# Expert 0's first row numbers from one-hot matmuls, and the later lists read behind the gathers, in a fused attention and mixture-of-experts kernel

## The chip, the cores and the metric

The kernel runs on one core of one Trainium2 chip. The metric is the device time of one execution in microseconds; a program is judged by the median of its runs. TensorE (PE) multiplies matrices, with its weight load written PEld; VectorE is DVE, ScalarE is ACT, GpSimd is POOL, and SyncE (SP) issues the plain DMAs. Each engine works through its own instructions strictly in order, so an instruction that waits holds up everything behind it on that engine.

## The reference, cut to what matters

```python
x = attention(q, k, v)                      # 2304 tokens of 512
x = relu(x @ w_in) ** 2 @ w_out             # dense layer, 512 -> 2048 -> 512
logits = x @ w_gate                         # 8 experts
e_idx = argmax(logits, axis=1)              # one expert for each token
gate_w = softmax(logits)[e_idx]
eom = 1 / (1 + exp(-(x @ w_output_gate)))
for e in range(8):
    mask = e_idx == e
    h = relu(x[mask] @ w1[e])               # 512 -> 1024
    out[mask] = gate_w[mask] * eom[mask, e] * (h @ w2[e])
```

With the inputs used here the experts 0 to 7 get 87, 361, 162, 89, 231, 520, 500 and 354 tokens.

## The kernel before, in words

Attention comes first, then the dense layer in nine chunks of 256 tokens, and behind each chunk its routing (`routing(c)`): the chosen expert, the token's rank in that expert and the gate value. Every token's result row of 520 numbers, gate included, is written to a table in DRAM (`ytab`, line 607). Its row number (`row`, 1 to 2304) is scattered to a place in DRAM lists (`orders`, line 601, two lists, one for the even and one for the odd 128 tokens of a chunk; both start as zeros, so their sum is the list). Expert e's list begins at place 2304e; `sc[:, 5, :]` holds each token's place as a float.

The expert stage needs the rows of one expert gathered in tiles of 128. One expert is chosen early as the lead (`star`, the fullest one after seven chunks; here expert 5). Its first FT = 2 tiles are gathered with the lists as they stand before the last chunk (`lead_rows`, called at step f = 6 of the last chunk) and are worked on as `fill` work (`lead_1` is layer 1, `lead_2` turns the hidden values and runs layer 2) while the last chunk's routing runs. `fill` is driven in steps of one matmul.

After the last routing, lines 958 to 973 read expert 0's list back from DRAM (`c4`), add the two lists (`cf`), step over the lead's two tiles if expert 0 should be the lead (`cd`, `star`), make integers (`ci`), and gather expert 0's first two tiles (`xg01`). Lines 979 to 983 and 999 to 1021 read all lists (`og`), turn them on TensorE (`po`) and make the integer places of all further tiles (`gi`). Line 996 holds the first three weight loads of expert 1 on SP behind the `c4` DMAs. `ph1.close()` gives up the buffers of the first phase, and the tiles of pool `mp2`, weight stages 3 to 7 among them, lie in that memory.

Then the loop over experts (line 1108): layer 1 of the tile in `xs0`, the weights of the next expert converted to two parts and loaded, rows of the next tiles gathered (`gather`, line 1041), turned and split (`split_rows`), the hidden values turned (`hand_over`), and at the end `tc.If(nt[e] > 1)` (line 1155). Where an expert has one tile, as expert 0 has, the other branch is taken. The first tile of the next expert (`xgs[0]`) is gathered by line 1097 before the loop. Layer 2 of a tile runs behind layer 1 of the next.

The instruction order on each engine is set ahead of time by a scheduler that simulates the program; `tc.high_priority()` moves work forward in it, and `tc.issue_after(x)` keeps instructions behind x on x's engine.

Of the kernel before, what the change touches and what calls it, by code (L numbers as in the profile page):

```python
# [10 lines left out]
F32 = mybir.dt.float32  # L11
F32R = mybir.dt.float32r
BF16 = mybir.dt.bfloat16
I32 = mybir.dt.int32
# [11 lines left out]
def attn_moe_kernel(  # L26
# [13 lines left out]
    nc = tc.nc  # L40
# [489 lines left out]
    def routing(c):  # L530
# [171 lines left out]
    def lead_rows():  # L702

        of = const.tile([P, 2, FT], F32, name="of")
        for i, o in enumerate(orders):
            nc.sync.dma_start(out=of[:, i, :], in_=lists(o)[bass.ds(most["e"], 1), :, 0:FT].rearrange(
                "o p t -> (o p) t"))
        oi = const.tile([P, FT], I32, name="oif")
        nc.vector.tensor_add(out=oi, in0=of[:, 0, :], in1=of[:, 1, :])
        xe = late.tile([P, FT, YW], F32, tag="xe", name="xe")  # L710
# [4 lines left out]
        most["xe"] = xe  # L715

    def lead_split():
        xs = mp.tile([P, FT, 2, DM], F32R, tag="xc", name="xsf")
# [18 lines left out]
    def lead_2(x):  # L737
# [3 lines left out]
        for h in range(2):  # L741
            t = psh.tile([P, DM], F32, tag="ph", name=f"ptf{x}_{h}")
            for c in range(4):
                f0 = 512 * h + P * c
                nc.tensor.transpose(out=t[:, P * c:P * c + P], in_=most["hr"][:, f0:f0 + P],
                                    identity=ident)
                yield
            nc.scalar.activation(out=hs[2 * h], in_=t, func=AF.Copy)
            nc.vector.tensor_sub(out=hs[2 * h + 1], in0=t, in1=hs[2 * h].bitcast(F32))
# [200 lines left out]
    for part, n in (("yt", 10), ("lg", 4), ("ps", 9)):  # L950
        route(1)
        with tc.issue_after(most[part]):
            drive(fill, n)
    route(8)


    star = most["star"]
    with tc.high_priority():
        c4 = const.tile([P, 2, 2 * FT], F32, name="c4")
        for i, o in enumerate(orders):  # L960
            got = nc.sync.dma_start(out=c4[:, i, :], in_=lists(o)[0, :, 0:2 * FT])
        cf = const.tile([P, 2 * FT], F32, name="cf")
        nc.vector.tensor_add(out=cf, in0=c4[:, 0, :], in1=c4[:, 1, :])
        cd = const.tile([P, FT], F32, name="cd")
        nc.vector.tensor_sub(out=cd, in0=cf[:, FT:], in1=cf[:, 0:FT])
        ci = const.tile([P, FT], I32, name="ci")
        nc.vector.scalar_tensor_tensor(out=ci, in0=cd, scalar=star[:, 0:1], in1=cf[:, 0:FT],
                                       op0=ALU.mult, op1=ALU.add)
        xg01 = [late.tile([P, YW], F32, tag=f"xg{i}", name=f"xg0{i}") for i in range(2)]
        for i in range(2):  # L970
            nc.gpsimd.indirect_dma_start(
                out=xg01[i][:], out_offset=None, in_=ytab[:],
                in_offset=bass.IndirectOffsetOnAxis(ap=ci[:, i:i + 1], axis=0))
# [4 lines left out]
    ogs = []  # L978
    for o in orders:
        og = cv.tile([P, DM], I32, tag="tmp", name="og", bufs=TMPB).bitcast(F32)[:E * NTL // 2, 0:2 * P]  # L980
        nc.gpsimd.dma_start(out=og.rearrange("t (h p) -> t h p", h=2),
                            in_=o.rearrange("(t h p) o -> t h (p o)", h=2, p=P))
        ogs.append(og)
    cs = counts("c")
    nti = const.tile([P, E], I32, name="nti")
    nc.vector.tensor_copy(nti, cs)
# [12 lines left out]
    po = psa.tile([P, 2, DM], F32, tag="at", name="po")  # L999
    for h in range(2):  # L1000
        for i, og in enumerate(ogs):
            with tc.issue_after(most["end"]):
                nc.tensor.matmul(po[:, 0, h * E * NTL // 2:(h + 1) * E * NTL // 2],
                                 lhsT=og[:, P * h:P * h + P],
                                 rhs=ident[:E * NTL // 2, :E * NTL // 2], start=(i == 0), stop=(i == 1))
    gi = late.tile([P, E * NTL // 2, 2], I32, tag="gi", name="gi")

    HT = NTL // 2
    pov = po[:, 0, 0:E * NTL].rearrange("p (h e j) -> p h e j", h=2, e=E)
    gih = gi.rearrange("p (e j) h -> p h e j", e=E)  # L1010
    sh = cv.tile([P, DM], F32, tag="tmp", name="sh", bufs=TMPB)[:, 0:E * (NTL - 2)].rearrange(
        "p (h e j) -> p h e j", h=2, e=E)
    nc.vector.tensor_copy(gi, po[:, 0, 0:E * NTL].rearrange("p (h t) -> p t h", h=2))
    for h in range(2):
        nc.vector.tensor_sub(out=sh[:, h], in0=pov[:, h, :, 1:HT], in1=gih[:, h, :, 0:HT - 1])
        nc.vector.tensor_tensor(out=sh[:, h], in0=sh[:, h],
                                in1=star.unsqueeze(2).to_broadcast([P, E, HT - 1]),
                                op=ALU.mult)
        nc.vector.tensor_tensor(out=gih[:, h, :, 0:HT - 1], in0=pov[:, h, :, 0:HT - 1], in1=sh[:, h],
                                op=ALU.add)  # L1020
    giv = gi.rearrange("p t h -> p (t h)")
    ph1.close()


# [9 lines left out]
    xs0 = mp2.tile([P, 2, DM], F32R, tag="xs0", name="xs0", bufs=1)  # L1034
    early[3] = mp2.tile([P, 1024], F32, tag="stg3", name="stg3", bufs=1)
    hr = most["hr"]
    g1, gn, gp = (mp2.tile([P, 2], F32, tag=f"g{i}", name=f"g{i}", bufs=1) for i in range(3))
    stages += [early[i] for i in range(3, 8)]

# [68 lines left out]
    for e in range(E):  # L1108
# [2 lines left out]
        n = f"{e}_0"  # L1111
        nt[e] = nc.values_load(nti[0:1, e:e + 1], min_val=0, max_val=NTL)
        first_mm = layer1_here(w1v, xs0, n)
        if more:
            after = experts[e + 1]
            after.place(0)
            with ExitStack() as behind:
                if e == 0:
                    for x in first_xs:
                        behind.enter_context(tc.issue_after(x))  # L1120
                for i in range(4):
                    after.split(i)
            for i in range(4, 8):
                after.load(i, stages[i])
# [99 lines left out]
```

## Time and profile before

| | us |
|---|---|
| median of 3 runs | 904.06 (900.21 to 905.27) |
| the profiled execution | 903.22 |
| its span | 901.4 |
| PE busy in the span | 821.4 (91%) |
| DVE, ACT, POOL busy | 450.6, 395.3, 341.6 |

Times in the rows are counted from the start of the span. A row of the timeline is one or more instructions of one line; the square bracket behind it is the idle time of that engine just before, and what ended it. SPq and PEq are the engines' sequencers, which run register, branch and DMA-issuing instructions; a sequencer can be ahead of its engine's array. [...]

### The profile page before, as it was taken

What the parts mean: (1) busy time and instruction counts of PE and PEld (TensorE: products, weight loads), DVE (VectorE), ACT (ScalarE), POOL (GpSimd) and SP (SyncE); (2) the same over time, 40 slices, a digit from 0 to 9 for tenths busy, and PEclk for the clock granted to TensorE, in tenths of its full rate; (3) what the DMA queues carried; (4) which work ended last, traced back from release to release, by engine and by line L of the source; (5) the groups of instructions that cost most, each with busy time, mean ns of one, the idle gap of its engine ahead of it and who ended that gap; (6) DMA issues with size and microseconds to landing.
All of it is one profiled execution on the core that took longest, in us unless ns stands there. A gap on an engine that the chain in (4) does not pass through costs nothing. (4 is left out here: it accounts for less than half of the span.)

```text
span 901.4 us, 15844 instructions
## 1 busy us (share of the span) xinstructions
PE 821.4 (91%) x5983; PEld 695.4 (77%) x5983; DVE 450.6 (50%) x961; ACT 395.3 (44%) x899; POOL 341.6 (38%) x411
## 2 busy tenths in 40 slices
PE   4598979997899989999999999997799989999996
PEld 3386869886788878888988888775587767878785
DVE  8987585777354654353222224652743656434121
ACT  3644555554434443344333324552643656444221
POOL 4556454454344445453323232413422332221111
PEclk9989989999899999999999999998899999999999
DMA  9750321454034332010000031635945594431111
GB/s 335 254 179 31 117 80 71 164 187 163 24 102 79 79 101 65 30 38 30 1 25 1 1 95 55 207 110 152 355 148 191 172 347 137 177 132 37 49 35 35
DMA packets 35519, 103.45 MB, mean 115 GB/s; under 512 B 6836, under 2 KB 6864, under 8 KB 35408
## 3 DMA queue, kind: packets, MB, share of 16 engines
q1 hardware_dynamic: 30000, 87.16, 28.9%
q0 software_dynamic: 5408, 14.88, 5.4%
q8 instruction: 61, 1.00, 0.5%
q14 instruction: 50, 0.41, 0.2%
HBM read 88.16 MB, written 14.65 MB: 114 GB/s over the span
## 5 line engine op out<-in xcount | busy, mean ns | idle before, releaser
L461 PE MATMUL ph<-xc,win 128*128 128x256 f32 x1728 | 244.6, 288 | 14.1 <-DVE g L466 11.9
L461 PEld LDWEIGHTS ph<-xc,win 128*128 128x128 f32 x1728 | 230.0, 193 | 33.4 <-DVE g L466 14.8
L484 PE MATMUL y<-wout,gs 128*128 128x512 f32 x864 | 233.0, 401 | 5.0 <-ACT gs L469 4.1
L470 POOL TENSOR_TENSOR gs<-g,gs 128x256 fp32r<-128x256 f32 x144 | 111.8, 780 | 201.1 <-ACT gs L469 123.7
L484 PEld LDWEIGHTS y<-wout,gs 128*128 128x128 f32 x864 | 152.7, 190 | 34.8 <-ACT gs L469 5.1
L466 DVE SCALAR_TENSOR_TENSOR g<-ph,g 128x256 f32<-128x256 f32 x144 | 60.2, 420 | 173.0 <-ACT g L465 172.8
L465 ACT ACTIVATE g<-ph 128x256 f32<-128x256 f32 x144 | 54.7, 382 | 121.7 <-PE ph L461 101.2
L469 ACT ACTIVATE gs<-g 128x256 fp32r<-128x256 f32 x144 | 59.5, 415 | 60.5 <-DVE g L466 55.1
L794 PE MATMUL ph<-we_wa,xs 128*128 128x512 f32 x228 | 64.3, 417 | 16.2 <-PEq L1155 10.7
L1041 POOL DMA_INDIRECT xg<-ytab,apt x23 | 33.2, 1442 | 88.2 <-ACT apt L799 44.4
L794 PEld LDWEIGHTS ph<-we_wa,xs 128*128 128x128 f32 x228 | 42.4, 195 | 28.4 <-ACT we_wd L657 11.1
L794 PE MATMUL ph<-we_wb,xs 128*128 128x512 f32 x228 | 60.3, 399 | 0.6 <-issue 0.6
L1082 DVE COPY g<-g 128x2 f32<-128x2 f32 x19 | 3.2, 168 | 104.0 <-ACT ob L1073 104.0
L1069 PE MATMUL py<-we_wc,hs 128*128 128x512 f32 x216 | 54.2, 399 | 0.0
L1069 PE MATMUL py<-we_wd,hs 128*128 128x512 f32 x216 | 53.4, 396 | 0.0
L794 PEld LDWEIGHTS ph<-we_wb,xs 128*128 128x128 f32 x228 | 43.6, 191 | 11.7 <-issue 1.1
L1073 ACT ACTIVATE ob<-py,g 128x512 f32<-128x512 f32 x18 | 12.4, 687 | 88.4 <-PE py L1069 78.5
L1076 POOL DMA_INDIRECT out_dram<-ob,oi x18 | 18.6, 1034 | 82.6 <-issue 36.2
L1069 PEld LDWEIGHTS py<-we_wd,hs 128*128 128x128 f32 x216 | 40.6, 188 | 9.8
L1069 PEld LDWEIGHTS py<-we_wc,hs 128*128 128x128 f32 x216 | 39.8, 188 | 8.7
L799 ACT ACTIVATE apt<-ph 128x512 f32<-128x512 f32 x38 | 22.9, 601 | 45.2 <-PE ph L794 45.2
L448 DVE TENSOR_TENSOR xc<-xT,xc 128x256 fp32r<-128x256 f32 (+3 forms) x76 | 37.0, 537 | 2.8 <-ACT xc L447 2.8
(258 smaller groups left out, 1217.4 us busy)
## 6 DMA issues: line engine op xcount, KB each, us to landing
apt<-in_w_dram SPq DMA_DIRECT2D x37, 512.0 KB, 3.1
stg<-in_w_dram SPq DMA_DIRECT2D x35, 512.0 KB, 7.6
apt<-in_qk_dram SPq DMA_DIRECT2D x10, 576.0 KB, 4.3
raw<-in_w_out_dram SPq DMA_DIRECT2D x11, 512.0 KB
raw<-in_w_in_dram SPq DMA_DIRECT2D x11, 512.0 KB, 3.3
ytab<-yr SPq DMA_DIRECT2D x18, 260.0 KB, 2.3
yr<-ypart SPq DMA_DIRECT2D x8, 512.0 KB, 4.2
sparewb<-in_qk_dram SPq DMA_DIRECT2D x6, 576.0 KB, 13.1
```

Source lines behind the costliest of these rows:

```text
L448: nc.vector.tensor_sub(out=t[:, 1, hp, done:done + ln], in0=src, in1=hi.bitcast(F32))
L461: nc.tensor.matmul(ph, lhsT=wv[:, wh, kk, :], rhs=x[:, xh, kk, :], start=(n == 0), stop=(n == 3 * KC - 1))
L465: nc.scalar.activation(out=g, in_=ph, func=AF.Relu)
L466: nc.vector.scalar_tensor_tensor(out=g, in0=ph, scalar=0.0, in1=g, op0=ALU.max, op1=ALU.mult)
L469: nc.scalar.activation(out=gs[:, 0, :], in_=g, func=AF.Copy)
L470: nc.gpsimd.tensor_sub(out=gs[:, 1, :], in0=g, in1=gs[:, 0, :].bitcast(F32))
L484: nc.tensor.matmul(yps[c][i], lhsT=gs[:, gh, P * i:P * i + P], rhs=woutv[f // FQ][:, f % FQ, wh, :], start=(first and n == 0), stop=(last ...
L794: mm = nc.tensor.matmul(ph, lhsT=xs[:, a, P * kk:P * kk + P], rhs=w1v(b, kk)[:, 512 * h:512 * h + 512], start=(n == 0), stop=(n == 3 * KC ...
L799: nc.scalar.activation(out=hr[:, 512 * h:512 * h + 512], in_=ph, func=AF.Relu)
L1041: nc.gpsimd.indirect_dma_start(out=xg[:], out_offset=None, in_=ytab[:], in_offset=bass.IndirectOffsetOnAxis(ap=idx, axis=0))
L1069: nc.tensor.matmul(py, lhsT=hs[:, a, P * kf:P * kf + P], rhs=w2v(b, kf), start=(kf == 0 and n == 0), stop=(kf == KF - 1 and n == 2))
L1076: nc.gpsimd.indirect_dma_start(out=out, out_offset=bass.IndirectOffsetOnAxis(ap=oi[:, 0:1], axis=0), in_=ob[:], in_offset=None, bounds_che ...
```

## The change

The list of expert 0 as it stands before the last chunk is read in `lead_rows`, where the lead's own list is read, and kept as a float (`had`). In the last routing, VectorE compares each token's place with the numbers 0 to 255 (`places`), which gives two one-hot tiles of 128x256 (`hits`), and four matmuls with a single column carry the row numbers of the last chunk to their places. The sum of that and `had` is `ci`. The read of `c4` after the last routing is gone; six steps of `fill` stand ahead of the four matmuls and 35 behind (39 before). The read of all lists moves behind expert 0's two gathers, into tiles of `mp2`; turning them (`places()`) and the gather of expert 1's first tile move behind the last matmul of expert 0's layer 1. The loads of expert 1's weights no longer stand behind the `c4` DMAs, the splits of `feed(16)` stand behind `ci`, and expert 0's `split_rows` stands behind the lead's last hidden values (`most["hs"]`).

```diff
@@ routing
+        if c == NCH - 1:
+            last_rows(c, sc[:, 5, :])
@@ lead_rows
+        c4 = const.tile([P, 2, 2 * FT], F32, name="c4")
+        for i, o in enumerate(orders):
+            nc.sync.dma_start(out=c4[:, i, :], in_=lists(o)[0, :, 0:2 * FT])
+        cf = const.tile([P, 2 * FT], F32, name="cf")
+        nc.vector.tensor_add(out=cf, in0=c4[:, 0, :], in1=c4[:, 1, :])
+        cd = const.tile([P, FT], F32, name="cd")
+        nc.vector.tensor_sub(out=cd, in0=cf[:, FT:], in1=cf[:, 0:FT])
+        nc.vector.scalar_tensor_tensor(out=cd, in0=cd, scalar=most["star"][:, 0:1], in1=cf[:, 0:FT],
+                                       op0=ALU.mult, op1=ALU.add)
+        places = late.tile([P, FT * P], F32, tag="places", name="places")
+        nc.gpsimd.iota(places, pattern=[[1, FT * P]], base=0, channel_multiplier=0,
+                       allow_small_or_imprecise_dtypes=True)
+    def last_rows(c, dest):
+        at = const.tile([P, 2], F32, name="at")
+        off = const.tile([P, 1], F32, name="off")
+        nc.vector.tensor_scalar(out=off, in0=most["star"][:, 0:1], scalar1=float(FT * P), ...)
+        nc.vector.tensor_scalar(out=at, in0=dest, scalar1=off[:, 0:1], ...)
+        for i in range(2):
+            h = mp.tile([P, CH], F32, tag="g", name=f"hit{i}")
+            nc.vector.tensor_scalar(out=h, in0=most["places"], scalar1=at[:, i:i + 1], scalar2=None,
+                                    op0=ALU.is_equal)
+    def last_places(c):
+        pn = psa.tile([P, 2, DM], F32, tag="at", name="pn")
+        for x in range(FT):
+            for i, h in enumerate(most["hits"]):
+                most["rk"] = nc.tensor.matmul(pn[:, 0, x:x + 1], lhsT=h[:, P * x:P * x + P],
+                                              rhs=row[:, 2 * c + i:2 * c + i + 1],
+                                              start=(i == 0), stop=(i == 1)).ins
+        ci = const.tile([P, FT], I32, name="ci")
+        most["ci"] = nc.vector.tensor_add(out=ci, in0=pn[:, 0, 0:FT], in1=most["had"]).ins
@@ after route(8)
+    with tc.issue_after(most["rk"]):
+        drive(fill, 6)
-        (c4, cf, cd and ci from the lists)
+        ci = last_places(NCH - 1)
@@
-        drive(fill, 39)
-    with tc.issue_after(most["routed"]), tc.issue_after(most["lt"]):
+        drive(fill, 35)
+    with tc.issue_after(most["ci"]), tc.issue_after(most["lt"]):
         feed(16)
@@
-    with tc.issue_after(most["routed"]), tc.issue_after(got.ins):
+    with tc.issue_after(most["routed"]):
         for i in range(3):
             experts[1].load(i, stages[i])
@@ og, po, gi move from here into mp2
+        with tc.issue_after(got):
+            nc.gpsimd.dma_start(out=og.rearrange("t (h p) -> t h p", h=2), ...)
@@ ahead of the loop
-    first_xs = split_rows(xgs[0], xs0, g0, "0_0")
-    gather(xgs[0], index(1, 0))
+    with tc.issue_after(most["hs"]):
+        first_xs = split_rows(xgs[0], xs0, g0, "0_0")
@@ in the loop
         first_mm = layer1_here(w1v, xs0, n)
+        if e == 0:
+            with tc.issue_after(first_mm), tc.high_priority():
+                places()
+                gather(xgs[0], index(1, 0))
```

`layer1_here` returns its last matmul.

## Rows read from the trace of the kernel before

**Rows 1.** Stretches: us; PE, PEld, DVE, ACT, POOL busy; granted clock, DMA share, GB/s.
```profile
586.00:606.00 20.00, 19.92 (x113) 16.05 (x112) 10.91 (x25) 12.44 (x25) 2.92 (x3) 1.00 0.30 102
606.00:616.20 10.20, 9.64 (x45) 7.39 (x44) 3.44 (x11) 2.27 (x5) 3.42 (x3) 1.00 0.30 59
616.20:620.70 4.50, 0.03 (x1) 0.03 (x1) 1.64 (x9) 0.00 (x0) 1.45 (x2) 0.65 0.64 181
638.20:644.70 6.50, 0.04 (x1) 0.07 (x1) 6.50 (x9) 4.58 (x5) 1.20 (x1) 0.75 1.01 376
685.40:901.40 216.00, 199.82 (x944) 161.18 (x944) 85.26 (x136) 90.89 (x136) 51.59 (x56) 0.98 0.39 136
```
**Rows 2.** Timeline, from the last chunk's places to the first stall's end.
```profile
607.12 0.17 DVE L595 CAST di<-rsc 128x2 int32<-128x2 f32 x1
607.57 1.83 POOL L601 DMA_INDIRECT order<-row,di  x1 [13.09 <-DVE di L595]
612.59 4.36 SPq L961 DMA_DIRECT2D c<-order  x2
616.99 1.45 SPq L648 DMA_DIRECT2D apt<-in_w_dram  x3
618.92 0.16 DVE L963 TENSOR_TENSOR cf<-c 128x4 f32<-128x4 f32 x1 [9.37 <-DMA c<-order]
619.81 1.03 POOL L971 DMA_INDIRECT apt<-ytab,ci  x1 [2.11 <-DVE nti L986]
620.67 4.28 PE L756 MATMUL pyf<-we-1_wc,hsf 128*128 128x512 f32 x10 [4.48 <-DVE hsf L749]
624.79 2.96 PE L756 MATMUL pyf<-we-1_wd,hsf 128*128 128x512 f32 x12
```
**Rows 3.** Timeline, lists, expert 0's layer 1 and the second stall.
```profile
627.58 1.01 PE L1003 MATMUL po<-ident,og 72*128 72x72 f32 x8
628.63 0.31 DVE L1013 CAST apt<-po 128x144 int32<-128x144 f32 x1 [2.47 <-PE po L1003]
629.72 1.19 PE L794 MATMUL ph<-we_wa,xs 128*128 128x512 f32 x4 [0.69 <-ACT xs L1054]
630.14 0.23 DVE L1019 TENSOR_TENSOR apt<-po,sh 128x64 int32<-128x64 f32 x1
630.50 0.99 POOL L1041 DMA_INDIRECT apt<-ytab,apt  x1 [0.74 <-issue]
634.45 1.57 PE L794 MATMUL ph<-we_wb,xs 128*128 128x512 f32 x6
637.48 0.20 DVE L1056 COPY g<-apt 128x2 f32<-128x2 f32 x1 [5.25 <-DMA apt<-ytab,apt]
644.66 2.90 PE L794 MATMUL ph<-we_wa,xs 128*128 128x512 f32 x6 [6.52 <-PEq L1155]
```
**Rows 4.** Branches of PE's sequencer: count, min/median/max ns, first and last start.
```profile
L1155 PEldq COMPARE_BRANCH  x8: 77/82/6359, 638.1 to 859.7; - x8
L1156 PEldq COMPARE_BRANCH  x17: 65/193/3794, 668.7 to 887.9; - x17
```
**Rows 5.** A gather in quiet queues, and DMA's share from 665.8 to 670 (40 slices).
```profile
665.84 1.15 POOL L1041 DMA_INDIRECT xg<-ytab,apt  x1 [3.08 <-ACT apt L799]
DMA  0000000000000000008185896494261320000000
```
**Rows 6.** Groups of like instructions: busy us, mean ns.
```profile
L390 DVE TENSOR_SCALAR cvt<-cvt 128x512 int32<-128x512 int32 x32 | 18.3, 573 | 14.8 <-ACT cvt L389 14.4
L556 PE MATMUL lg<-psum,lgt 128*128 128x16 f32 x36 | 4.7, 244 | 0.0
```
**Rows 7.** Timeline where `lead_rows` runs: its DMAs, the loads behind, who waits.
```profile
573.46 1.95 SPq L706 DMA_DIRECT2D of<-order  x2
580.22 1.06 ACT L657 ACTIVATE we-1_wc<-apt 128x1024 fp32r<-128x1024 f32 x1 [3.50 <-DMA apt<-in_w_dram]
580.75 2.06 PE L484 MATMUL y<-wout,gs 128*128 128x512 f32 x6 [0.40 <-POOL gs L470]
```

More of the change, by code (lines that the diff above doesn't have):

```diff
@@ L709, in lead_rows @@
         nc.vector.tensor_add(out=oi, in0=of[:, 0, :], in1=of[:, 1, :])
+        c4 = const.tile([P, 2, 2 * FT], F32, name="c4")
[10 more added lines that the diff above has]
+                       allow_small_or_imprecise_dtypes=True)
+        most.update(had=cd, places=places)
         xe = late.tile([P, FT, YW], F32, tag="xe", name="xe")
@@ L748, in lead_2 @@
             nc.scalar.activation(out=hs[2 * h], in_=t, func=AF.Copy)
-            nc.vector.tensor_sub(out=hs[2 * h + 1], in0=t, in1=hs[2 * h].bitcast(F32))
+            most["hs"] = nc.vector.tensor_sub(out=hs[2 * h + 1], in0=t, in1=hs[2 * h].bitcast(F32)).ins
         if x == 0:
@@ L954, in attn_moe_kernel @@
     route(8)
+    with tc.issue_after(most["rk"]):
+        drive(fill, 6)
     star = most["star"]
     with tc.high_priority():
[L959 to L968, printed above, removed]
+        ci = last_places(NCH - 1)
         xg01 = [late.tile([P, YW], F32, tag=f"xg{i}", name=f"xg0{i}") for i in range(2)]
         for i in range(2):
-            nc.gpsimd.indirect_dma_start(
+            got = nc.gpsimd.indirect_dma_start(
                 out=xg01[i][:], out_offset=None, in_=ytab[:],
-                in_offset=bass.IndirectOffsetOnAxis(ap=ci[:, i:i + 1], axis=0))
+                in_offset=bass.IndirectOffsetOnAxis(ap=ci[:, i:i + 1], axis=0)).ins
     with tc.issue_after(most["rk"]):
-        drive(fill, 39)
-    with tc.issue_after(most["routed"]), tc.issue_after(most["lt"]):
+        drive(fill, 35)
+    with tc.issue_after(most["ci"]), tc.issue_after(most["lt"]):
         feed(16)
[L978 to L983, printed above, removed]
     cs = counts("c")
@@ L995, in attn_moe_kernel @@
     stages = [late.tile([P, 1024], F32, tag="stg", name=f"stg{i}", bufs=3) for i in range(3)]
-    with tc.issue_after(most["routed"]), tc.issue_after(got.ins):
+    with tc.issue_after(most["routed"]):
         for i in range(3):
             experts[1].load(i, stages[i])
[L999 to L1021, printed above, removed]
     ph1.close()
@@ L1036, in attn_moe_kernel, with places @@
     hr = most["hr"]
+    ogs = []
+    for o in orders:
+        og = mp2.tile([P, 2 * P], F32, tag=f"og{len(ogs)}", name="og", bufs=1)[:E * NTL // 2, :]
+        with tc.issue_after(got):
+            nc.gpsimd.dma_start(out=og.rearrange("t (h p) -> t h p", h=2),
+                                in_=o.rearrange("(t h p) o -> t h (p o)", h=2, p=P))
+        ogs.append(og)
+    gi = late.tile([P, E * NTL // 2, 2], I32, tag="gi", name="gi")
+    giv = gi.rearrange("p t h -> p (t h)")
+    def places():
+        po = ps2.tile([P, DM], F32, tag="py", name="po", bufs=2)
+        for h in range(2):
+            for i, og in enumerate(ogs):
+                nc.tensor.matmul(po[:, h * E * NTL // 2:(h + 1) * E * NTL // 2],
+                                 lhsT=og[:, P * h:P * h + P],
+                                 rhs=ident[:E * NTL // 2, :E * NTL // 2], start=(i == 0), stop=(i == 1))
+        HT = NTL // 2
+        pov = po[:, 0:E * NTL].rearrange("p (h e j) -> p h e j", h=2, e=E)
+        gih = gi.rearrange("p (e j) h -> p h e j", e=E)
+        sh = mp2.tile([P, E * (NTL - 2)], F32, tag="sh", name="sh", bufs=1).rearrange(
+            "p (h e j) -> p h e j", h=2, e=E)
+        nc.vector.tensor_copy(gi, po[:, 0:E * NTL].rearrange("p (h t) -> p t h", h=2))
+        for h in range(2):
+            nc.vector.tensor_sub(out=sh[:, h], in0=pov[:, h, :, 1:HT], in1=gih[:, h, :, 0:HT - 1])
+            nc.vector.tensor_tensor(out=sh[:, h], in0=sh[:, h],
+                                    in1=star.unsqueeze(2).to_broadcast([P, E, HT - 1]),
+                                    op=ALU.mult)
+            nc.vector.tensor_tensor(out=gih[:, h, :, 0:HT - 1], in0=pov[:, h, :, 0:HT - 1],
+                                    in1=sh[:, h], op=ALU.add)
     g1, gn, gp = (mp2.tile([P, 2], F32, tag=f"g{i}", name=f"g{i}", bufs=1) for i in range(3))
```

7 lines of the change are left out of this document (added).

## The prediction

> **What bounds the kernel now.** I read the stretches first, to see where PE, busy for 91% of the span, is not busy. In the dense layer it has no gaps worth the name: 19.92 of 20 us in the last stretch before the change's place. Between the last routing and expert 1 there are two stalls: 4.5 us from 616.2, in which PE is busy for 0.03 us, and 6.5 us from 638.2, with 0.04 us; behind them PE is again busy for 199.8 of 216 us [rows 1]. So the change is decided in some 40 us, and what it wins there is kept, because from expert 1 on each tile follows the last at PE's own pace.
>
> The timeline around the first stall shows its cause. The last chunk's places are integers at 607.12, the scatter to the lists goes out from 607.57, the two reads of expert 0's list leave SP at 612.59 and 616.56 (a start of 612.59 and a length of 4.36 for two), and VectorE, which stands at `cf`, gets the second at 618.92, having idled 9.37 us. Behind `cf` on the same engine stand the low halves of the lead's hidden values, and those are what PE waits for until 620.67 [rows 2]. So PE waits neither for the gather nor for the list, but for work queued behind a wait on the list.
>
> The second stall is read from its end. The bracket of the matmul at 644.66 names PE's sequencer at line 1155, not data [rows 3], and that line's branch on PE once lasted 6,359 ns and has a median of 82 [rows 4]. Ahead of that branch PE's queue holds the transposes of expert 1's first tile, whose gather went out at 630.50 and landed just before 637.48, where VectorE stops idling for it [rows 3]. From that landing to the restart it is 7.2 us: 6.4 in the branch, which begins at 638.1, and 0.8 around it [rows 4]. The chain is thus lists, gather, branch, restart.
>
> The sum is made against the profiled execution, 903.22 us with 1.8 us outside its span; the median of the three runs is 904.06, 0.8 us above it. Changes are carried to the median unaltered.
>
> **Part 1, the read back is removed.** PE's wait of 4.48 us goes. So does what follows it: after the stall ten matmuls take 4.28 us where twelve of the same kind take 2.96 [rows 2], at a granted clock that stood at 0.65 in the stall's stretch [rows 1], so partly at the lower level; ten at the full rate are 2.47, and 1.8 us are won. The turning of the lists moves from in front of expert 0's layer 1 to behind it: the lead's last matmul ends at 624.79 + 2.96 = 627.75 and layer 1 starts at 629.72 [rows 2, 3], 1.97 us, of which I leave 0.6 for the four transposes of expert 0's tile; 1.4 won. Its gather, which went out at 619.81 [rows 2], can go out when POOL has finished the two scatters (at most two times 1.83 us from 607.57, so by about 611), and lands under the lead's layer 2. Sum of part 1: 4.5 + 1.8 + 1.4 = 7.7 us.
>
> **Part 2, the one-hot work is added on PE and DVE.** The trace has no comparison of this form and no matmul with one column. The nearest rows are 573 ns for a tensor-scalar of twice the width, so some 0.3 us each for two, and 244 ns for a matmul of 16 columns, overlapped in part, so 0.5 to 1.0 us for four [rows 6]. VectorE has the place as a float at 607.1, so the one-hot tiles are there at about 608.1; the six `fill` steps put ahead end at about 607.8. PE loses 0.3 us of waiting and 0.7 of work: 1.0, between 0.5 (all but the matmuls hidden) and 1.5. The splits put behind `ci` are needed only by expert 0's layer 2, and nothing is late for them. Expert 0's layer 1, which ended at 634.45 + 1.57 = 636.02 [rows 3], then ends 6.7 us earlier; I say 6.5, for a third stall of 0.2 at the hidden values' low half.
>
> **Part 3, the list as it stands before the last chunk is read earlier.** Two more DMAs of 512 numbers of 4 bytes stand on SP behind the two of the lead's list (573.46 to 575.41), ahead of weight loads. ACT waits 3.50 us for one of those loads at 580.22, and PE, fed by ACT and POOL, waits 0.40 us right behind [rows 7], so this stretch has no cover left for ACT. Three DMAs in a row leave SP in 1.45 us [rows 2], so the loads move by 1.0 us of issue and by the time that 1,024 small pieces take in the queue. I take 1.0 us of loss on PE; the ends are 0 (the scheduler puts other ACT work first) and 2.5.
>
> **Part 4, the places of the further tiles and the gather of expert 1's first tile now wait for layer 1's end.** This is what is late next. Before, the gather left 5.5 us ahead of that end and lay beside layer 1. Now, from layer 1's end: turning 1.05 us (627.58 to 628.63), DVE's seven operations 1.74 (628.63 to 630.37), POOL's start 0.13 [rows 3]: 2.9 us. Then the gather. In quiet queues it takes 3.4 us (issued 665.84; the DMA share falls to nothing some 32 slices of 0.105 us behind 665.8) [rows 5]; in full ones it took 6.9 (630.50 to 637.4) [rows 3]. Then the branch with what leads to it: 7.2 us in full queues, where the DMA share was 1.01 [rows 1]; the other long ones end at 3.8 [rows 4], which with 0.8 is 4.6. Expert 1's first three loads are no longer behind the lists (616.99 [rows 2]), and stages 3 to 7 no longer wait for the lists' buffers, so most of that traffic should be over. I take values near the quiet ends, 4.0 and 5.1. The chain is 2.9 + 4.0 + 5.1 = 12.0 us where it was 644.66 - 636.02 = 8.64: 3.4 us given back.
>
> Removing this wait thus moves the bound from PE's own order to a chain of DMAs. PE idles longer there than before, and it will restart at the lower clock as before (six matmuls took 2.90 us at 644.66 against 1.57 for six at 634.45 [rows 3]); I leave that term as it is, with 1.8 us either way.
>
> On the branch, the trace shows 6.4 us with full queues and at most 3.8 elsewhere [rows 1, 4]. [...]
>
> [...]
>
> **Sum.** -6.5 + 1.0 + 3.4 = -2.1 us, so 901.1 on the profiled execution and 902.0 against the median. Quiet ends: -7.0 + 0 + (2.9 + 3.4 + 4.6 - 8.64 = 2.3) = -4.7, 899.4. Loaded ends: -6.0 + 2.5 + (2.9 + 6.9 + 7.2 - 8.64 = 8.4) = +4.9, 909.
>
> **The rivals.** First, everything falls quiet: the chain runs with empty DMA queues, part 3 costs nothing, and part of the lower clock's 1.8 us goes as well. That is 899.4 down to 897.6, and I say 898.5. For it: the weights go out up to 10 us earlier. Against: four more loads of expert 1 still wait for the lead's end, and expert 2's follow them.
>
> Second, slower: the chain of part 4 takes the place of both stalls. The place is the gather of expert 1's first tile and the branch behind it; their price is 14.1 us loaded against the 9.1 I take. With 1.0 us lost in part 3, the change loses from the point where gather and branch together pass 8.64 + 5.5 - 2.9 = 11.2 us. Loaded as before, that gives -6.5 + 1.0 + 8.4 = +2.9, 907. For it: in the row where PE stalled the queues were full, and the eight loads remain eight. Against: they start earlier.
>
> Third, the change does not do what it says: expert 0's gather is held by something else (the table's writes, POOL's scatters, the weight loads that now go ahead of it) and layer 1 starts no earlier, while part 4 is paid: +1.0 + 3.4, 908.5. Against: the DMA share was 0.30 from 606 to 616.2 [rows 1], and layer 2 of the lead gives the gather some 10 us of cover.
>
> **How the numbers follow.** Forecast 0.53 (902.0), quiet 0.25 (898.5), loaded chain 0.17 (907), nothing won 0.05 (908.5). Half a per cent, about what a measurement of this kernel can tell from no change, is 4.5 us: under 899.5 lie the quiet rival and a little of the forecast, 0.30; above 908.6 the loaded ends and part of the third, 0.11; between them 0.59. The range leaves out the far end of either side: 897.8 to 907.5.
>
> **What would show it.** Right: no wait of PE on the lead's hidden values near 616; layer 1 of expert 0 ending near 629.5; PE then idle for 8 to 10 us, ended by line 1155's branch (or its successor), which begins under 1 us behind the landing of expert 1's gather; that gather leaving about 2.9 us behind layer 1's end. Part 3: ACT's wait near 580 longer than 3.5 us, and PE's dense layer ending about 1 us later. [...]

## The result and the profile after

The changed kernel takes 908.84 us (906.77 to 913.55) where the kernel before, on the same chip, takes 903.98 (900.21 to 905.74): a ratio of 1.0061, 95% interval 1.0037 to 1.0084. It is 0.6% slower; forecast were 902.0, and 897.8 to 907.5 as the range. The profiled execution after took 907.45 us with a span of 905.5, against 903.22 and 901.4.

Timeline of the changed kernel on TensorE, the place of the change (start, us, engine and line, count, idle time before and what ended it), to be laid beside [rows 2, 3]. `layer1` is now line 837, the jump over expert 0's further tiles line 1199:

```profile
610.24 0.35 PE L753 MATMUL pn<-row,hit 128*128 128x1 f32 x2
618.95 3.33 PE L799 MATMUL pyf<-we-1_wc,hsf 128*128 128x512 f32 x12 [0.39 <-ACT hsf L791]
626.34 2.13 PE L837 MATMUL ph<-we_wa,xs 128*128 128x512 f32 x8 [0.83 <-ACT xs L1094]
630.64 1.57 PE L837 MATMUL ph<-we_wb,xs 128*128 128x512 f32 x6
633.54 0.79 PE L1059 MATMUL po<-ident,og 72*128 72x72 f32 x6
640.53 1.09 PE L1092 MATMUL px<-ident,apt 128*128 128x128 f32 x4 [6.20 <-DMA apt<-ytab,apt]
645.36 2.90 PE L837 MATMUL ph<-we_wa,xs 128*128 128x512 f32 x6 [3.74 <-PEq L1199]
```

The first stall of [rows 2], 4.48 us, is down to 0.39, and the lead's layer 2 starts at the full granted clock (1.00 from 618.95; twelve in 3.33, where [rows 2] has ten in 4.28). Expert 0's layer 1 ends at 630.64 + 1.57 = 632.21. Behind it TensorE idles 6.20 and 3.74 us, where [rows 3] has 6.52. The other engines there, as in [rows 2, 3]:

```profile
609.54 0.16 DVE L597 CAST di<-rsc 128x2 int32<-128x2 f32 x1
612.68 1.98 POOL L1007 DMA_INDIRECT apt<-ytab,ci  x1 [0.30 <-issue]
634.04 0.68 DVE L1131 TENSOR_TENSOR hs<-pt,hs 128x512 fp32r<-128x512 f32 x1
634.63 0.30 DVE L1068 CAST apt<-po 128x144 int32<-128x144 f32 x1
634.85 0.68 DVE L1131 TENSOR_TENSOR hs<-pt,hs 128x512 fp32r<-128x512 f32 x1
636.97 1.00 POOL L1081 DMA_INDIRECT apt<-ytab,apt  x1 [7.56 <-issue]
640.42 0.17 DVE L1096 COPY g<-apt 128x2 f32<-128x2 f32 x1 [3.59 <-DMA apt<-ytab,apt]
```

Expert 0's first rows are fetched from 612.68, 3.14 us behind the row numbers (609.54), where [rows 2] has 12.7. Further back, at expert 4, stands a wait that the kernel before has not. TensorE's timeline there, and the stretch as in [rows 1] (us; busy time of PE, PEld, DVE, ACT, POOL; granted clock, DMA share, GB/s):

```profile
730.70 1.19 PE L837 MATMUL ph<-we_wa,xs 128*128 128x512 f32 x2 [4.19 <-PEq L1199]
734.54 1.86 PE L837 MATMUL ph<-we_wa,xs 128*128 128x512 f32 x4 [2.65 <-DVE we_wa L660]
...
728.50:738.80 10.30, 5.45 (x13) 4.11 (x14) 9.24 (x9) 6.56 (x7) 4.36 (x3) 0.50 0.85 292
```

The same place of the kernel before, timeline and stretch:

```profile
730.37 2.90 PE L794 MATMUL ph<-we_wa,xs 128*128 128x512 f32 x6 [4.16 <-PEq L1155]
...
728.50:738.80 10.30, 8.43 (x30) 6.79 (x31) 8.97 (x9) 7.47 (x9) 4.73 (x3) 0.83 0.92 330
```

Six matmuls in a row there; here two, 2.65 us of nothing, then four, with the granted clock at 0.50 through the stretch, against 0.83. The third matmul multiplies the same half of the weights as the first, and its other operand, the low half of the rows, was written by 728.5; so it is no wait for data, whatever the bracket infers. What TensorE does get in that time, as I read it, is a piece of its code: one of the packets of queue q8, whose kind is instruction (63 packets, 1.03 MB in this profile, 16 KB each). The DMA row of 731.6 to 733.4 (queue, packets, MB, share of 16 engines):

```profile
q8 instruction: 1, 0.02, 5.9%
```

The packet runs from 731.63 to 733.34, and the third matmul starts 1.2 us behind its end.

A last pair belongs to `lead_rows` [rows 7]. VectorE of the kernel before, then VectorE and TensorE of the changed one:

```profile
577.25 0.16 DVE L709 TENSOR_TENSOR oif<-of 128x2 int32<-128x2 f32 x1 [0.98 <-DMA of<-order]
```

```profile
580.85 0.16 DVE L711 TENSOR_TENSOR oif<-of 128x2 int32<-128x2 f32 x1 [2.21 <-DMA of<-order]
581.81 0.16 DVE L717 TENSOR_TENSOR cf<-c 128x4 f32<-128x4 f32 x1 [0.74 <-DMA c<-order]
582.55 1.68 PE L461 MATMUL ph<-xc,win 128*128 128x256 f32 x12 [1.26 <-DVE g L466]
```

VectorE idles for the lead's row numbers and then for the new list; TensorE waits for the dense layer's `g`, which stands behind both on VectorE. SP had issued the new reads (line 715) between the two of the lead's rows (line 708) and behind them; two of the four:

```profile
575.92 0.46 SPq L715 DMA_DIRECT2D c<-order  x1
577.20 0.38 SPq L708 DMA_DIRECT2D of<-order  x1
```

To compare many profiles I cut each at four instructions of its timeline: `di` of chunk 7, `di` of the last chunk, the first matmul of expert 1, and the last instruction. Differences in us:

| profile | start to chunk 7 | last chunk | to expert 1 | to the end | ratio of times (95%) |
|---|---|---|---|---|---|
| before | 568.45 | 38.67 | 37.54 | 256.73 | |
| changed | 570.47 | 39.07 | 35.82 | 260.09 | 1.0061 (1.0037 to 1.0084) |
| again | 567.99 | 41.13 | 35.63 | 260.42 | 1.0047 (1.0024 to 1.0071) |
| after_pad20 | 569.34 | 39.93 | 35.81 | 258.91 | 1.0054 (1.0035 to 1.0072) |
| after_pad40 | 569.74 | 43.43 | 35.73 | 256.13 | 1.0037 (1.0020 to 1.0055) |
| before_pad10 | 571.83 | 38.78 | 36.37 | 257.64 | 1.0027 (1.0014 to 1.0040) |
| before_pad30 | 571.22 | 39.06 | 37.28 | 261.11 | 1.0025 (1.0009 to 1.0041) |
| before_pad80 | 571.30 | 38.70 | 37.09 | 256.56 | 1.0003 (0.9983 to 1.0024) |
| before_c4 | 570.28 | 41.52 | 36.81 | 256.96 | 1.0038 (1.0019 to 1.0057) |
| late_c4 | 569.69 | 39.99 | 35.67 | 259.17 | 1.0039 (1.0019 to 1.0059) |
| places_first | 571.36 | 39.54 | 35.32 | 259.45 | 1.0081 (1.0059 to 1.0103) |
| places_mid | 571.08 | 39.66 | 34.84 | 259.94 | 1.0039 (1.0023 to 1.0055) |
| clean | 572.50 | 39.00 | 35.33 | 257.08 | 0.9989 (0.9973 to 1.0006) |
| best | 572.22 | 38.88 | 34.41 | 256.17 | 0.9993 (0.9976 to 1.0011) |

Between the first two rows lie +2.02, +0.40, -1.72 and +3.36: 4.06 us, the difference of the spans.

### The profile page after: what moved, and what is told of

Its sections match the earlier page's. It is cut to its first block, busy times and chain, and to the rows that moved or that the text cites. A ratio compares the mean times of both kernels' runs of the same rounds, so it can differ in the third digit from the quotient of the medians.

```text
span 905.5 us, 15866 instructions
## 1 busy us (share of the span) xinstructions
PE 823.6 (91%) x5991; PEld 697.3 (77%) x5991; DVE 453.0 (50%) x966; ACT 394.2 (44%) x899; POOL 336.0 (37%) x412
## 3 DMA queue, kind: packets, MB, share of 16 engines
q8 instruction: 63, 1.03, 0.5%
## 5 line engine op out<-in xcount | busy, mean ns | idle before, releaser
L1081 POOL DMA_INDIRECT xg<-ytab,apt x23 | 28.8, 1254 | 90.0 <-ACT apt L842 44.4
```

What stands on the lines that cost most here:

```text
L1081: nc.gpsimd.indirect_dma_start(out=xg[:], out_offset=None, in_=ytab[:], in_offset=bass.IndirectOffsetOnAxis(ap=idx, axis=0))
```

## Experiments

**The changed kernel once more.** No edit.

> The changed kernel, nothing altered. Theory: behind expert 3's jump, TensorE runs out of the 16-KB instruction packet six instructions into expert 4 and stands until the next one is there; that belongs to the program and comes again: the third matmul of expert 4 with a wait of 2 to 3.5 us ahead of it, behind a jump wait of about 4.2 us. Rival: it was one disturbed execution, and then the wait is gone and the span 3 to 4 us shorter than 905.5. The 1.9 us that the profiled execution had lost by chunk 7, where both programs are the same, is expected to come out otherwise (between 0 and 2). Median 907 to 910 against about 904 for the kernel before.

```profile
730.02 1.19 PE L837 MATMUL ph<-we_wa,xs 128*128 128x512 f32 x2 [3.61 <-PEq L1199]
733.51 1.86 PE L837 MATMUL ph<-we_wa,xs 128*128 128x512 f32 x4 [2.30 <-DVE g L1096]
```

TensorE's timeline: the wait came again, behind the same two matmuls, and this time another instruction of VectorE is named for it. Median 910.45. Chunk 7 was reached at 567.99, 2.5 us sooner than in the first profile of the same program; over all profiles this first stretch lies between 567.99 and 572.50, with the two orders mixed. So the first 2.02 us of the difference are none of the change's.

**Code that never runs, in the changed kernel.**

```diff
         def block(j):
             ...
+            if e == 1 and j == 5:
+                pad = ps3.tile([P, DM], F32, tag="px", name="pad", bufs=2)
+                for _ in range(10):          # 20 instructions; 20 for 40
+                    nc.tensor.transpose(out=pad[:, 0:P], in_=ident, identity=ident)
```

Expert 1 has three tiles, so the block for its sixth is jumped over. In all five runs with such a pad the instructions that do run, and their order on TensorE, VectorE, ScalarE and GpSimd, are those of the kernel without it.

> The changed kernel with 20 TensorE instructions more (10 transposes) in expert 1's block for a sixth tile, which is never executed: all code behind it lies 20 instructions further on. Theory (instruction packets): expert 4's entry then lies behind the packet's end and comes with the jump, the wait of 2 to 3.5 us at its third matmul is gone, and the kernel is 2.5 to 4 us faster than the changed one: 905 to 906.5. Rival (the split weights we_wa, or their loads, come late at expert 4): code that never runs moves no weights, the wait stays, 908.8.

> The changed kernel with 40 never executed TensorE instructions in place of 20. Theory (instruction packets): with 20 the packet's end moved away from expert 4's entry and on to expert 6's, where the third matmul then waited 1.71 us. The two lie 16 to 20 instructions apart, so with 40 both ends lie ahead of the entries: no wait at experts 2, 4 and 6 behind the 0.92 us (or 3.7 us, far jump) of the jump itself; from expert 1's start to the end the profile takes 256 to 257 us, as against 260.1 in the changed kernel and 258.9 with 20. Rival (late weights): a wait of 2 us stays at one of them.

Timeline of TensorE with 20, at expert 4 and at expert 6, then with 40 at expert 4:

```profile
729.55 1.85 PE L837 MATMUL ph<-we_wa,xs 128*128 128x512 f32 x6 [3.71 <-PEq L1203]
...
796.88 0.73 PE L837 MATMUL ph<-we_wa,xs 128*128 128x512 f32 x2 [0.92 <-ACTq L1204]
799.33 1.87 PE L837 MATMUL ph<-we_wa,xs 128*128 128x512 f32 x4 [1.71 <-issue]
```

```profile
733.97 2.90 PE L837 MATMUL ph<-we_wa,xs 128*128 128x512 f32 x6 [4.64 <-PEq L1203]
```

Twenty unexecuted instructions took the wait away from expert 4 and put one at expert 6. With 40 there is none, and the stretch from expert 1 to the end is 256.13 us, inside the 256 to 257 expected. The rival, late weights, falls. By the ratios the gain is smaller than by the profiles: with 20 the median, 909.69, missed the 905 to 906.5 expected and no gain shows; with 40 it is 0.1 to 0.24%, 1 to 2 us, within the intervals. And with the wait gone the kernel is still slower than the one before, by 0.37% (0.20 to 0.55). That profile has the longest last chunk of all, 43.43 us.

**The same in the kernel before.** The edit with 5, 15 and 40 transposes.

> The kernel before with 10 TensorE instructions more (5 transposes) in the same block, never executed: that many more instructions precede expert 4's entry in the changed kernel than in the kernel before. Theory (instruction packets): the wait of 2 to 3.5 us shows in the kernel before too, at expert 4's third matmul or thereabouts, and it becomes 2.5 to 4 us slower: 906.5 to 908. Rival (late weights, or the rest of the change): no wait there, 904.

> The kernel before with 30 never executed TensorE instructions. With 10 the packet's end moved from behind the eighth matmul of expert 2 to behind its third, five matmuls or ten instructions, exactly as padded, and expert 4 kept its head start; so the changed kernel's code lies about 30 instructions further on than the one before, not 10. Theory (instruction packets): with 30 the end is ahead of expert 2's entry and the wait of 0.62 us there goes; at expert 4 it falls behind the second to fifth matmul, with a wait of 1.5 to 2.7 us there and the lower clock behind it, so that expert 1's start to the end takes 258.5 to 260.5 us instead of 256.7 and the ratio is 1.001 to 1.004. Rival: the wait at expert 4 belongs to the changed order of work; then it doesn't show, and that stretch takes 255.8 to 256.7 us.

> The kernel before with 80 never executed TensorE instructions. Theory: the packet's end moves from the ninth matmul of expert 2 to ahead of its entry, and the wait of 0.62 us there is gone with the lower clock behind it: 0.5 to 1 us faster than before, no other wait longer, ratio 0.998 to 1.000. Rival: code that never runs costs time by itself, as the run with 10 instructions seemed to (ratio 1.0027 where its profile shows 0.9 us more): ratio 1.002 or more.

The kernel before has a small wait of the kind at expert 2; its timeline, then that with 10 instructions more, then that with 30 at expert 4:

```profile
685.45 1.66 PE L794 MATMUL ph<-we_wa,xs 128*128 128x512 f32 x6 [0.92 <-ACTq L1156]
686.94 0.62 PE L794 MATMUL ph<-we_wb,xs 128*128 128x512 f32 x2
688.19 1.20 PE L794 MATMUL ph<-we_wb,xs 128*128 128x512 f32 x4 [0.62 <-issue]
```

```profile
688.13 0.96 PE L794 MATMUL ph<-we_wa,xs 128*128 128x512 f32 x3 [0.92 <-ACTq L1160]
690.78 0.97 PE L794 MATMUL ph<-we_wa,xs 128*128 128x512 f32 x3 [1.69 <-issue]
```

```profile
732.36 1.06 PE L794 MATMUL ph<-we_wa,xs 128*128 128x512 f32 x3 [4.16 <-PEq L1159]
737.05 1.65 PE L794 MATMUL ph<-we_wa,xs 128*128 128x512 f32 x3 [3.63 <-issue]
```

Ten instructions (each transpose is a weight load and a matmul; TensorE's page has 5,983 of either) moved the wait from behind the eighth matmul to behind the third: five pairs, exactly the pad. My expectation for expert 4 failed there, since I had put the shift between the two kernels at 10 instructions. With 30 the wait stands at expert 4 of the kernel before, behind three matmuls where the changed kernel has two (so the shift is about 32), 3.63 us long and with nothing named for it, and expert 1 to the end takes 261.11 us, even above the 258.5 to 260.5 expected. That settles it: the wait belongs to where the code lies, not to what the change does. With 80 the wait at expert 2 is gone, but one at the start of the last block, 0.92 us in the kernel before, has grown:

```profile
891.17 3.06 PE L1069 MATMUL pyend<-we_wc,hs 128*128 128x512 f32 x12 [2.01 <-issue]
```

so "no other wait longer" was wrong, and nothing was gained (1.0003). The measured ratio with 30, 1.0025, is 2.3 us, while the profile shows 4.4 more from expert 1 to the end; that execution is the second longest of its twelve, and how far the wait varies was not measured. With 10 it is the other way round: the ratio, 1.0027, is 2.4 us, and the profile shows 0.9 more behind expert 1. That code which never runs costs time by its mere presence isn't borne out: with 80 the ratio is 1.0003.

**The indices ahead of layer 1.**

```diff
-        first_mm = layer1_here(w1v, xs0, n)
-        if e == 0:
-            with tc.issue_after(first_mm), tc.high_priority():
-                places()
-                gather(xgs[0], index(1, 0))
+        if e == 0:   # read: the last po matmul; behind: an ExitStack around layer 1 (cut)
+            with tc.issue_after(first_xs[1]), tc.high_priority():
+                read, done = places()
+                gather(xgs[0], index(1, 0))
+            behind.enter_context(tc.issue_after(read))
+        first_mm = layer1_here(w1v, xs0, n)
```

> The changed kernel with one part undone: the index matmuls, the arithmetic of gi and the gather of expert 1's rows stand ahead of expert 0's layer 1 (as in the kernel before) instead of behind it, the lists still read behind the gathers. Theory: the chain behind layer 1's end (13.15 us to expert 1's first matmul) is what the change gave back; with the gather under layer 1 only jump and fetch stay, about 6 to 8.5 us, so expert 1 starts 4.5 to 7 us earlier (near 639 to 641) and the kernel takes 902 to 904.5. Rival: the lists land too late behind the gathers, TensorE waits for them ahead of layer 1 instead, and layer 1 ends as much later as the chain gets shorter: 907 to 909.

```profile
629.01 0.44 PE L1059 MATMUL po<-ident,og 72*128 72x72 f32 x2 [2.15 <-DMA og<-order]
630.41 2.90 PE L837 MATMUL ph<-we_wa,xs 128*128 128x512 f32 x6
646.21 2.04 PE L837 MATMUL ph<-we_wa,xs 128*128 128x512 f32 x4 [6.56 <-PEq L1202]
```

The rival held, and more: TensorE waits 2.15 us for the lists ahead of layer 1, which then starts at the lower clock (six in 2.90), and the jump takes 6.56 us instead of 3.74. Expert 1 starts 35.32 us behind the row numbers, half a microsecond better than in the changed kernel; the time is not better. Its median, 912.15, is the longest of all runs, and its one profile, the shortest of its six executions, doesn't show why.

**The indices inside layer 1.** First half, indices, second half.

```diff
+            for mm in half_layer1(w1v, xs0, ph[0], hr, 0): pass
+            with tc.issue_after(mm), tc.high_priority():
+                read, done = places()
+                gather(xgs[0], index(1, 0))
+            with tc.issue_after(read):
+                for first_mm in half_layer1(w1v, xs0, ph[1], hr, 1): pass
```

> The changed kernel with the index matmuls and the gather of expert 1's rows between the two halves of expert 0's layer 1 (first half, then the indices, then the second half). The lists landed at 629.0 in the run that had them ahead of layer 1, so they are there after the first half. Theory: the gather then flies under the second half, TensorE reaches the jump some 5 us earlier and restarts 2 to 5 us earlier than in the changed kernel (33.0 to 33.8 us after the last chunk's row numbers instead of 35.8 at the most): 906 to 908. Rival: the jump's instruction packet comes later when the gathers and loads fill the queues beside it (jump waits 6.5 us as in the kernel before, not 3.7), expert 1 starts where it did, 35 to 36 us after the row numbers, and the time stays at 909 to 910.

```profile
640.86 1.09 PE L1093 MATMUL px<-ident,apt 128*128 128x128 f32 x4 [3.32 <-DMA apt<-ytab,apt]
645.58 2.90 PE L837 MATMUL ph<-we_wa,xs 128*128 128x512 f32 x6 [3.63 <-PEq L1207]
```

34.84 us, between the two theories: the gather left only at 635.88, behind the splits on VectorE, and landed 4.9 us later. The jump stayed at 3.63, so what makes it 6.5 is not the gather's own place. The DMA rows of the four microseconds behind the jump's start (queue: packets, MB, share of 16 engines) show what goes with it. First the kernel before, jump from 638.1, then the changed one, from 641.1:

```profile
q1 hardware_dynamic: 267, 0.98, 62.7%
q0 software_dynamic: 157, 0.50, 34.8%
```

```profile
q0 software_dynamic: 248, 0.82, 72.7%
q8 instruction: 1, 0.02, 1.8%
q14 instruction: 3, 0.02, 1.5%
```

q1 carries the weight loads: three of 512 KB are issued in the first of these windows, none in the second. Beside the weights of the kernel before, the packet of q8 is in 5.0 us behind the jump's start, in the changed kernel 2.3. The branch takes 6.36, 6.76 and 6.24 us in the kernel before, with the indices ahead, and in before_c4 (267, 244 and 257 packets of q1), and 3.98, 3.94 and 3.64 in the changed kernel, with the indices inside, and in clean (no packet of q1).

**Part 3 alone, and part 3 later.** First the two reads and their three sums, unused, in the kernel before; then the changed kernel with the reads behind both of the lead's and one load, and the sums behind the last row numbers.

```diff
 def lead_rows():            # before_c4
+        c4x = const.tile([P, 2, 2 * FT], F32, name="c4x")
+        for i, o in enumerate(orders):
+            nc.sync.dma_start(out=c4x[:, i, :], in_=lists(o)[0, :, 0:2 * FT])
+        ...                 # cfx, cdx as cf, cd
```

```diff
 def last_chunk(f):          # late_c4
         if f == 12:
             feed(6)
+            with tc.issue_after(most["ld"]):     # the last load
+                lists_of_0()                     # the two reads
 def last_places(c):
+        with tc.issue_after(most["routed"]):
+            had()                                # cf, cd
```

> The kernel before with part 3 of the change alone: the two early reads of expert 0's lists and the three sums on them are there, and nothing uses them. Theory: VectorE's wait for the loaded expert's rows grows from 0.9 to between 2 and 4 us, the last chunk takes 39.1 to 41.1 us instead of 38.7, and the kernel is 0.5 to 2.5 us slower than before. Rival: the wait belongs to another part of the change; it stays below 1.2 us and the time is that of the kernel before.

> The changed kernel with its part 3 taken back half way: the two reads of expert 0's lists are issued behind both reads of the loaded expert's rows and one load, and the three small sums that use them stand behind the last chunk's row numbers on VectorE, not ahead of its splits. Theory: in the four profiles with these reads in front, VectorE waited 2.2 to 4.2 us for the loaded expert's rows and 0.4 to 0.7 us more for the lists, where the two profiles without them have 0.85 and 0.98; the last chunk took 39.1 to 41.1 us instead of 38.7. So the wait goes back to about 1 us, the last chunk to 38.7 to 39.0, and the kernel becomes 0.5 to 2.5 us faster than the changed one. Rival: the longer wait hangs on the state of the weight loads, not on these reads; then it stays at 2 to 4 us.

VectorE and TensorE of before_c4, then VectorE of late_c4:

```profile
582.43 0.16 DVE L709 TENSOR_TENSOR oif<-of 128x2 int32<-128x2 f32 x1 [4.52 <-DMA of<-order]
583.36 1.69 PE L461 MATMUL ph<-xc,win 128*128 128x256 f32 x12 [2.77 <-DVE g L466]
```

```profile
578.81 0.16 DVE L711 TENSOR_TENSOR oif<-of 128x2 int32<-128x2 f32 x1 [1.80 <-DMA of<-order]
```

Part 3 alone makes the kernel before slower, by 0.38%, and lengthens its last chunk by 2.85 us. Seven profiles with the early reads have last chunks of 39.07 to 43.43 us, mean 40.61; four of the kernel before without them 38.67 to 39.06, mean 38.80. So part 3 costs 1.8 us on the mean of the profiles, between 0.3 and 4.6; before_c4 itself lost more than expected, in the wait, in the last chunk and in time (0.38%, 3.4 us). With the reads one load later the lead's rows are no longer delayed: from the end of SP's issue to VectorE's sum it takes 1.77 us, as in the kernel before (1.84), against 3.26 in the changed one; the wait of 1.80 is there because VectorE comes earlier. But the last chunk still takes 39.99 and the ratio gains little; what costs there was not found.

**Both costs out, and then the chain.** `clean`: the reads behind four more loads (at f == 15), the sums behind the row numbers, and the pad of 40. `best`: the same, with the index matmuls behind the first six of layer 1 and the index arithmetic ahead of the last two splits.

```diff
 def last_chunk(f):          # clean and best; the sums as in late_c4, the pad as above
         if f == 15:
             feed(10)
+            with tc.issue_after(most["ld"]):
+                lists_of_0()
 for e in range(E):          # best, for e == 0
+            first = half_layer1(w1v, xs0, ph[0], hr, 0)
+            for _ in range(6): next(first)
+            read, done = places(most["l1"])      # behind the sixth matmul
+            gather(xgs[0], index(1, 0))
+            ...                                  # the rest of both halves, behind read
```

> The changed kernel with both found costs taken out: the two reads of expert 0's lists stand behind four more weight loads in SP's order and their sums behind the last chunk's row numbers, and 40 never executed TensorE instructions move the code (as in the run with 40). Theory (early reads +0.4 to +4.8 us in the last chunk, packet's end at expert 4 +3.7): last chunk 38.6 to 39.2 us, row numbers to expert 1 35.5 to 35.9, from there to the end 256.0 to 256.5, together some 2 us less than in the kernel before (332.9 from chunk 7's row numbers to the end): ratio 0.996 to 1.000, and faster than the changed kernel by 5 to 7 us. Rival: a further cost that these profiles don't show; ratio stays above 1.002.

> The same with the index matmuls behind the first six matmuls of expert 0's layer 1 and the arithmetic of the indices ahead of the last two splits on VectorE. Theory: the gather of expert 1's rows lands while the turned hidden rows are made, TensorE reaches the jump about 5 us earlier; the jump itself takes 4 us if the weight loads have run dry by then and 6 to 6.8 us if they fly beside it (6.36 in the kernel before, 6.76 with the indices ahead of layer 1, 3.98 and 3.94 where no load ran). So expert 1 starts 30.5 to 33.5 us after the row numbers instead of 35.7, ratio 0.992 to 0.998. Rival: the lists are not there after six matmuls and the wait moves into layer 1: 35 us or more, ratio as in the run without this.

Timeline of TensorE, clean at expert 4, then best at expert 1:

```profile
732.06 2.90 PE L846 MATMUL ph<-we_wa,xs 128*128 128x512 f32 x6 [3.88 <-PEq L1214]
```

```profile
639.86 0.63 PE L1107 MATMUL px<-ident,apt 128*128 128x128 f32 x4 [2.19 <-DMA apt<-ytab,apt]
645.52 2.90 PE L846 MATMUL ph<-we_wa,xs 128*128 128x512 f32 x6 [5.03 <-ACT we_wd L659]
```

clean takes 904.84 us against 905.61: 0.9989, 0.9973 to 1.0006. Against 1.0047 and 1.0061 for the changed kernel this is 0.58 and 0.72%, 5 to 6.5 us. So, within the intervals, the two costs are all of the loss, and without them the change is worth about 1 us (2.4 at the interval's end, and none at the other). From expert 1 to the end clean takes 257.08, a little more than the 256.0 to 256.5 expected. best brings expert 1 to 34.41 us instead of 35.33, short of the 33.5 hoped for, with a jump of 5.03 us between the two kinds; its time is not distinguishable from clean's. Its program is longer again, and a wait of the kind, 0.70 us with nothing named, stands in its last block at 890.96. Neither is shown to be faster than the kernel before.

What stays open: by the ratios the pad alone (1.0037) and the reads one load later alone (1.0039) win less than half of what clean wins; reads as late as in clean were never run without the pad. One reason may be in the record. The profiled executions of the seven kernels with the early reads all lie below the median of their runs, by 0.95 to 4.55 us and 2.4 on the mean; those of before_pad10, before_pad30, before_pad80, clean and best lie on both sides of it, 0.0 on the mean. So the profiles show too little of what part 3 costs. 1.8 and 2.4 make 4.2 us, and from after_pad40 to clean, which takes the early reads away, the ratios differ by 0.48%, 4.3 us. It fits, but it is an argument and no experiment.

## Why the prediction was wrong

**Parts 1 and 2 were right.** From the last row numbers to layer 1's end of expert 0 it was 636.02 - 607.12 = 28.90 us and is 632.21 - 609.54 = 22.67: 6.2 us less, forecast 6.5. The wait on the hidden values went as said, the gather left early, and the one-hot tiles held TensorE for about 1 us.

**Part 4 was mis-sized in its first term.** Layer 1's end to expert 1 is 13.15 us, forecast 12.0, before 8.64. The gather (636.97 to 640.42: 3.45, taken 4.0) and the jump with its surroundings (4.94, taken 5.1) were near the values taken. The turning and its arithmetic were not: 636.97 - 632.21 = 4.76 us instead of 2.9. I had costed them as they stood ahead of layer 1; behind it they share TensorE with the turning of the hidden values and VectorE with their splits, which stand between (634.04 and 634.85 above). Given back: 4.5 instead of 3.4. Over the profiles "to expert 1" gains 1.3 us on the mean (37.0 for five with the order of before, 35.7 for six with the change's), where 3.1 were forecast. One row was misread, without harm to the sum: 3.8 is the most that line 1156's branches take [rows 4], and line 1155 has a second long one, 5.94 us at 724.27 in the kernel before.

**Part 3 failed in its mechanism, and its term was too small.** I priced SP's issue and the small pieces ahead of weight loads, and looked at ScalarE, whose wait near 580 should have grown beyond 3.50 us. What grew is VectorE's wait for the lead's own row numbers, 0.98 us in the kernel before and between 2.21 and 4.52 where a new read stands between its two, and then for `cf`; behind both stand the products that feed TensorE. I had named this form of loss for the kernel before, work queued behind a wait on a list (the hidden values had been turned by 615.13, and their low halves were made only from 619.93, behind `cf`), and did not look for it where the change puts the same wait. Forecast 1.0, with 0 to 2.5; measured 1.8 on the mean of the profiles, up to 4.6, and 3.4 by the ratio of the run with part 3 alone (1.7 to 5.2).

**The step that was left out** is in the sentence that "what it wins there is kept, because from expert 1 on each tile follows the last at PE's own pace". From expert 1 to the end the changed kernel takes 260.09 and 260.42 us instead of 256.73, 3.5 more. The cause, as the runs with unexecuted code (ten instructions moved a wait by five matmuls) and the packets of q8 (one ends 1.2 us ahead of the restart at expert 4) show it, is that the added instructions move the later code against the 16-KB packets in which TensorE's instructions arrive, so that TensorE now waits 2.65 us for one behind the second matmul of expert 4. The forecast has no term and no chance for such a stall; yet the kernel before shows one of the kind, at 688.19 with 0.62 us and "issue" as its cause.

The sum by the means of the profiles is then +1.8 - 1.3 + 3.5 = +4.0 us; the medians differ by 4.9, and the ratio's interval is 3.3 to 7.6. By the ratios the shares lie otherwise: part 3 alone costs 3.4 us, and taking the wait away wins 1 to 2. So the wait is not what alone turned the sign: without it the kernel is still 0.37% slower, and part 3 alone already costs more than the 1 us that the change is worth without both. The third rival has nearly the measured time, 908.5, but for another reason: layer 1 did start earlier.

## What to carry to other kernels

Behind a jump, look for a wait that nothing explains ("issue", or a releaser that changes from run to run): here each of the five pads, of 10 to 80 instructions that never ran, moved such a wait or took one away, so try the edit with unexecuted code in one or two sizes before judging it by a few microseconds. One profile is one execution: here it lay up to 4.6 us off the median of its runs, so hold its stretches against the medians. A read moved ahead of its use was not free here while its first use stood in the middle of a busy engine's queue (0.38% for part 3 alone): move the use behind, too, and keep small reads from standing between the parts of one that is waited for (3.26 us to VectorE's sum where they did, 1.77 where not). Cost a step that moves with what shares its engines at the new place (4.76 us here), not with its duration at the old one (2.9).

## What the runs showed of the hardware

**TensorE's code.** Queue q8, of the kind instruction, moved 61 packets, 1.00 MB, in the profile before and 63, 1.03 MB, in the one after, 16 KB each. That TensorE's code arrives in them is read from the times: in both profiles each of TensorE's eight branches of over 1 us (3.3 to 6.4 us) ended 1.3 to 1.7 us behind the end of a packet of q8. One that came shortly behind a jump's target let TensorE stand: the profiles have eleven such waits, two to eight matmuls behind a jump; in each a packet of q8 has ended 1.1 to 1.5 us before TensorE goes on. Where the jump itself cost 0.92 us of TensorE, the wait was 0.62 with eight matmuls of head start, 1.69 with three and 1.71 with two; from the first matmul's start to that of the restart it is 2.74, 2.65 and 2.45 us, so the wait is what the head start leaves of some 2.6 us. At expert 4, where the jump cost 3.6 to 4.2 us, it was 1.92 to 3.04 with two matmuls (five profiles) and 3.63 with three, 3.1 to 4.7 us by the same count. The lower clock comes on top: 0.50 through the stretch at expert 4, against 0.83.

**The jumps' time went with the traffic beside them.** Over the fourteen profiles the 91 branches of over 1 us with no packet of the weight loads in their first four microseconds take 1.3 to 4.1 us, the 20 with 244 or more packets 5.4 to 6.8, and the one with 36 takes 4.9.

**The small reads delayed the small read beside them.** Two reads of 512 numbers of four bytes were issued beside the two of the lead's row numbers, one of them between these (the lists' reads are 2.0 KB each, the lead's 1.0; from 575 to 582 the changed kernel has 1,600 packets under 512 B). From the end of SP's issue of the lead's second read to VectorE's sum it is 3.26 to 5.06 us in the seven profiles with them, and 1.76 to 1.88 in the seven others. Whether their place, their number or their small pieces do it was not separated.
